# Weight stores move to the queue of loads, queries come one tile a slice, two copies go first, and loads and casts of the last stage change place

## The chip, the cores and the metric

The kernel runs on one core of one Trainium2 chip. The metric is the device time of one execution in microseconds (us). Three runs of the kernel before took 1599.2, 1599.79 and 1606.01 us; their median is 1599.79 us.

## The reference

Linear attention, and then two layers of the form "product, activation, product", all in float32:

```python
kv = einsum('bhsd,bhse->bhde', k, v)            # 8 x 8 heads, 576 positions, 64 wide
o = einsum('bhsd,bhde->bhse', q, kv)
x = o / sqrt(mean(o * o, -1) + 1e-6) * g_norm   # then 4608 tokens x 512
h = x @ moe_w_in                                # 512 x 2048
x = (h * sigmoid(h)) @ moe_w_out                # 2048 x 512
h = x @ moe2_w_in
out = (s * relu(h) ** 2 + b) @ moe2_w_out
```

The weights arrive as 64-bit floats. The kernel reads them as pairs of 32-bit integers and decodes them on ACT and DVE.

## The kernel before

Every large product is made of two float32r parts of each operand (`hi`, the cast; `lo`, the rest) and three passes: hi with hi, hi with lo, lo with hi. Four stages follow each other.

**First stage** (`emit_h`, line 470). Nine blocks of 512 tokens (j = 0 to 8), each in 16 slices (m). A slice is 12 matmuls into `ph`, a Silu on ACT (line 484), and beside them in `first_stage` the attention of block j + 1: kv products (line 349, m = 0 to 3), the transposes of the queries (`emit_qT`, line 364, m = 3 to 6), the output products and squares (`out_tile`, lines 374 to 428, m = 4 to 7), and the transposes into `xh` and `xl` (lines 442 to 447, m = 11 to 14). `load_next` (line 539) issues on SP the loads for that: four query tiles (line 357) in slices 0 and 1, keys and values of block j + 2 in slices 4 to 7. A query tile that crosses the border between two batches is loaded in two pieces.

**Weights of later stages.** From block 1 on, each slice also takes two or three steps of `weight_steps` for the weights of stages 2 and 3 (stage 4 follows during the third stage). Their products are made by the Strassen-Winograd scheme, seven products instead of eight, P1 to P7, and so each of 8 raw tiles gives seven combinations. `split` (line 228) writes a combination as `hi` (cast on ACT, line 235) and `lo` (subtraction on DVE, line 236) and puts off its store to DRAM by a slice or more with `defer` (line 237, issued by ACT). `run_late` issues what has come due. Raw weights are loaded by SP (lines 138 and 143) into two rooms, the next when its room has been decoded (`merge`, line 160).

**Second and fourth stage** (`Output`, matmuls at line 885). Five column blocks of 1024 tokens (the last, block 0, of 512), in units of one product and one quarter of the sum: 12 matmuls, six for each half q of the outputs. `load` brings tiles `r`, `sa` and `ka` of the activation from DRAM, `prepare` adds or subtracts them on DVE, `make` splits them (cast at line 808 on ACT, `lo` at line 810 on DVE), as a rule for the unit three ahead. After a product's last unit `end_of` takes the sums out of the banks. After P7 it copies y to `c` on ACT (line 860), adds v on DVE (line 861) and, in the last stage alone, scales it on ACT (`scaled`, line 821). The next product, P4, goes on in the bank y that was copied.

**Third stage** (`Hidden`, matmuls at line 677). For each of eight pairs of output tiles the seven products as slots of six matmuls, with copies and squares on ACT (lines 694 to 721) and sums on DVE; results go to `gt` in DRAM by stores that ACT issues (line 689). P4 and P3 come one pair late, so the last slots of the stage are P6, P3, P2, P7, P4, P3. `beside3` (line 963) puts beside the last block the loads of the last stage's weights (`grid[4].load`, line 312), the loads of its first activation tiles (`out4.load`) and their first casts (`out4.make`). `beside4` loads the rest of those weights, one in each unit, until 28 are there.

**What sets the order.** The order on every engine is that of the program text. An issue of a transfer stands in the stream of the engine that issues it, and can have to wait: for its data, for its room, or for the landing of an earlier transfer, as the profile's waits show. What stands behind it on that engine waits too.

Of the kernel before, what the change touches and what calls it, by code (L numbers as in the profile page):

```python
# [17 lines left out]
def kernel(  # L18
# [36 lines left out]
    nc = tc.nc  # L55
# [9 lines left out]
    TT = T // P  # L65
# [23 lines left out]
    def room(tag, shape, dtype, name):  # L89
        return sbuf.tile(shape, dtype, tag=tag, name=name)  # L90

    def bank(tag, name):
        return psum.tile([P, T], F32, tag=tag, name=name)
# [55 lines left out]
    def decode(stage, i, step):  # L149
        raw = raw_t[stage, i]  # L150
        low, high = raw[:, :, 0], raw[:, :, 1]
        if step == "rebias":
            nc.scalar.activation(high.bitcast(F32), high.bitcast(F32), AF.Copy, scale=REBIAS)
        elif step == "low":
            nc.vector.tensor_single_scalar(low, low, 29, op=ALU.logical_shift_right)
        elif step == "sign":
            nc.vector.scalar_tensor_tensor(low, high, SIGN, low, op0=ALU.bitwise_and, op1=ALU.bitwise_or)
        elif step == "merge":
            f = wf_t[stage, i] = room("wf_0", [P, WN], F32, f"wf{stage}_{i}")
            nc.vector.scalar_tensor_tensor(  # L160
                f.bitcast(I32), high, 3, low, op0=ALU.logical_shift_left, op1=ALU.bitwise_or
            )
# [25 lines left out]
    P1, P5, P6, P2, P7, P4, P3 = range(7)  # L188
    wd = {s: [[dram.tile([P, 2, T], F32, name=f"wd{s}_{k}_{a}") for a in range(NA)] for k in range(7)] for s in (2, 3, 4)}

    def quarters(stage, i):
        f = wf_t[stage, i]
        if stage % 2:
            f = f.rearrange("p (c h f) -> p c h f", c=KT, h=2)
            return f[:, 0:2, 0], f[:, 2:4, 0], f[:, 0:2, 1], f[:, 2:4, 1]
        f = f.rearrange("p (r h e) -> p r h e", r=2, h=2)
        return f[:, 0, 0], f[:, 1, 0], f[:, 0, 1], f[:, 1, 1]
# [3 lines left out]
    def weight_steps(stage, raws, sums_in, granule, slots, behind=None):  # L201

        made = {}
        turn = [0]

        def combine(i, part):
            a11, a12, a21, a22 = quarters(stage, i)
            if part == 0:
                if len(sums_in) == 1:
                    t = room(sums_in[0], [P, 4, 2 * P], F32, f"ws{stage}_{i}")  # L210
                    s = [t[:, n] for n in range(4)]
                else:
                    t = [room(tag, [P, 2, 2 * P], F32, f"ws{stage}_{i}_{tag}") for tag in sums_in]
                    s = [t[n // 2][:, n % 2] for n in range(4)]
                if stage % 2:
                    s = [x.rearrange("p (c f) -> p c f", c=2) for x in s]
                made[i] = dict(zip((P1, P2, P4, P5, P6, P7, P3), (a11, a12, a22, *s)))
                nc.vector.tensor_add(made[i][P5], a21, a22)
                nc.vector.tensor_sub(made[i][P6], made[i][P5], a11)
            elif part == 1:  # L220
                nc.vector.tensor_sub(made[i][P7], a11, a21)
                nc.vector.tensor_sub(made[i][P3], a12, made[i][P6])
            else:
                f = wf_t[stage, i].rearrange("p (r e) -> p r e", r=2)
                for r in range(2):
                    nc.vector.tensor_add(csum[0], csum[0], f[:, r])

        def split(i, k):
            src = made[i][k]
            to = granule(turn[0])  # L230
            turn[0] += 1
            hi, lo = to[:, 0], to[:, 1]
            if stage % 2:
                hi, lo = (x.rearrange("p (c f) -> p c f", c=2) for x in (hi, lo))
            nc.scalar.copy(hi, src)
            nc.vector.tensor_sub(lo, src, hi)
            defer(slots, lambda: nc.scalar.dma_start(
                wd[stage][k][i // 2][:, i % 2, :], to.bitcast(F32).rearrange("p s e -> p (s e)")
            ))

        def step(i, what):
            if i < NF:
                decode(stage, i, what)
                if what == "merge":
                    n = i + len(raws)
                    if n < NF:
                        load_raw(stage, n, raws[n % len(raws)])
                    elif behind:
                        load_raw(behind, n - NF, raws[n % len(raws)])

        def begin():
            if stage == 4:
                csum.append(room("gl_1", [P, T], F32, "csum"))
                nc.vector.memset(csum[0], 0.0)
            for i, tag in enumerate(raws):
                if (stage, i) not in raw_t:
                    load_raw(stage, i, tag)

        yield begin
        for what in ("rebias", "low", "sign", "merge"):  # L260
            yield lambda what=what: step(0, what)
        for i in range(NF):
            yield lambda i=i: combine(i, 0)
            yield lambda i=i: split(i, P1)
            yield lambda i=i: combine(i, 1)
            yield lambda i=i: split(i, P2)
            if stage == 4:
                yield lambda i=i: combine(i, 2)
            for k in (P4, P5, P6):
                yield lambda i=i, k=k: split(i, k)  # L270
            yield lambda i=i: step(i + 1, "rebias")
            yield lambda i=i: split(i, P7)
            yield lambda i=i: step(i + 1, "low")
            yield lambda i=i: split(i, P3)
            yield lambda i=i: step(i + 1, "sign")
            yield lambda i=i: step(i + 1, "merge")
# [4 lines left out]
    def defer(slots, f):  # L281
        late.append([slots, f])
# [71 lines left out]
    def load_q(t):  # L354
        a = q_pages[t % TT // 2][:, t % 2].rearrange("p (h d) -> p h d", h=H)
        for off, n, b, s in token_runs(t * P, P):
            nc.sync.dma_start(a[off:off + n], q[b, :, s:s + n, :].rearrange("h p d -> p h d"))
        q_t[t] = a
# [180 lines left out]
    def load_next(j, m):  # L539

        t0 = TT * (j + 1)
        if m < 2:
            load_q(t0 + 2 * m)
            load_q(t0 + 2 * m + 1)
        if 4 <= m < 4 + NP and j + 2 < B:
            load_kv(j + 2, m - 4)

# [188 lines left out]
    class Output:  # L736
# [109 lines left out]
        def end_of(self, b, k):  # L846
            n = size[b]
            x, y, v = ([self.acc.get((kind, q)) for q in range(2)] for kind in "xyv")
            for q in range(2):
                if k == P1:  # L850
                    self.acc["y", q] = bank(f"h_{q}", f"qy{self.stage}_{b}_{q}")
                    nc.scalar.copy(self.acc["y", q][:, :n], x[q][:, :n])
                elif k == P6:
                    self.acc["u", q] = room(U_ROOMS[q], [P, T], F32, f"qu{self.stage}_{b}_{q}")
                    nc.scalar.copy(self.acc["u", q][:, :n], y[q][:, :n])
                elif k == P2:
                    self.scaled(self.c_room(b, 0, q), x[q][:, :n], q)
                elif k == P7:
                    c = self.c_room(b, 1, 2 + q)
                    nc.scalar.copy(c, y[q][:, :n])  # L860
                    nc.vector.tensor_add(c, v[q][:, :n], c)
                    self.scaled(c, c, 2 + q)
                elif k == P4:
                    self.scaled(self.c_room(b, 0, 2 + q), y[q][:, :n], 2 + q)
                elif k == P3:
                    c = self.c_room(b, 1, q)
                    nc.vector.tensor_add(c, v[q][:, :n], self.acc["u", q][:, :n])
                    self.scaled(c, c, q)
            if self.stage == 4 and k in (P4, P3):
                self.waiting.extend((b, int(k == P3), r) for r in range(n // P))  # L870

# [46 lines left out]
    out2, hidden3, out4 = Output(2), Hidden(3), Output(4)  # L918
# [44 lines left out]
    def beside3(b, i, k):  # L963
        if b == order[0] and k in (P1, P4, P3, P7):
            grid[3].load()
        if b != order[-1]:
            if 0 < i < NF - 1 and k not in (P1, P3) and (i, k) != (NF - 2, P4):
                do_some(steps4, 1)
            return
        if i >= 3 and k in (P5, P2):  # L970
            grid[4].load()
        if i == 3 and k == P1:
            out4.load(2)
        if i == NF - 1:
            if k == P6:
                out4.load(4)
            if k in (P1, P5, P2, P7):
                out4.make({P1: 1, P5: 2, P2: 3, P7: 4}[k])

    def beside4(b, k, a):  # L980
        if b == order[0]:
# [126 lines left out]
```

## Time and profile before

| | |
|---|---|
| median of three runs | 1599.79 us |
| the profiled execution | 1600.95 us, of it 1599.2 us the span |
| granted clock of TensorE, mean | 0.997 |
| PE / DVE / ACT busy | 98% / 60% / 51% of the span |
| transfers | 349.58 MB, mean 219 GB/s |
| weight stores of stages 2 and 3 (`wd<-wo`, issued by ACT) | 112, 256 KB each, landing 3.8 us in the middle |
| query loads (`qp`, issued by SP) | 36, 28 of them of 256 KB |
| first / second / third / last stage begin at about | 36 / 528 / 877 / 1227 us |

PE is the engine that computes nearly the whole time; the other columns say how much the rest has to do beside it. In the rows, a bracket such as [2.59 <-ACT xh L446] means that the engine stood idle for 2.59 us before this instruction and that ACT's work of line 446 ended the wait. PEld is the weight load of TensorE. Names ending in q (ACTq, SPq) are an engine's issue of a transfer.

### The profile page before, as it was taken

Reading aid. Unit: us, or ns where it says so; the run is one execution under the profiler, and the core shown is the slowest. Engines: PE = TensorE matmul, PEld = TensorE weight load, DVE = VectorE, ACT = ScalarE, POOL = GpSimd, SP = SyncE. Lnnn points to the kernel's source line nnn. Section 1 sums busy time; section 2 is a strip of 40 time slices with the busy share of each in tenths; the row PEclk is TensorE's granted clock in tenths of the full one; section 3 lists DMA queues with packets and bytes.
Section 4 is the critical chain, followed back from the end, with each engine's and each line's share of the span. In section 5 each row is a group of like instructions: output and inputs, shape, how many; then the busy total and the mean of one; then the engine's idle time right before and its main releaser. Section 6 shows DMA issues by size and latency. Waiting matters only on the chain.

```text
span 1599.2 us, 21751 instructions
## 1 busy us (share of the span) xinstructions
PE 1569.1 (98%) x8232; PEld 1308.2 (82%) x8232; DVE 958.3 (60%) x1298; ACT 811.1 (51%) x1310; POOL 1.6 (0%) x8
## 2 busy tenths in 40 slices
PE   7999999999999999999999999999999999999998
PEld 4788887878888888888889788888888888888888
DVE  5635545545520758585858576767655757575845
ACT  3645554555432444444445565656555455555455
POOL 0000000000000000000000000000000000000000
PEclk9999999999999999999999999999999999999999
DMA  8977888798569763635349956574577862626251
GB/s 250 271 242 244 287 279 240 251 289 264 198 225 308 271 216 124 212 119 210 105 134 349 360 211 231 196 258 169 206 270 261 321 243 85 230 86 227 89 158 54
DMA packets 225609, 349.58 MB, mean 219 GB/s; under 512 B 56544, under 2 KB 94432, under 8 KB 225504
## 3 DMA queue, kind: packets, MB, share of 16 engines
q1 hardware_dynamic: 143936, 209.48, 40.9%
q10 hardware_dynamic: 81568, 138.71, 23.3%
q8 instruction: 65, 1.06, 0.3%
q14 instruction: 40, 0.33, 0.1%
HBM read 209.72 MB, written 138.41 MB: 218 GB/s over the span
## 4 chain that ended last, share of the span: by engine, by line
PE 88%; DMA 6%; ACT 2%; DVE 2%; issue 1%; ACTq 0%; SPq 0%; DVEq 0%
PE ph L470 23%; PE qy L885 16%; PE qx L885 12%; PE qv L885 11%; PE py L677 9%; PE pv L677 6%; PE px L677 6%; PE po L374 2%; PE pkv L349 2%; DMA r<-gt 1%; DMA w<-wd 1%; PE pt L837 1%; PE px L442 1%; DMA gt<-g 1%; PE pq L364 1%
## 5 line engine op out<-in xcount | busy, mean ns | idle before, releaser
L885 PE MATMUL qy<-o,w 128*128 128x512 f32 (+1 forms) x1440 | 300.3, 368 | 1.5 <-ACT c L860 1.5
L885 PEld LDWEIGHTS qy<-o,w 128*128 128x128 f32 x1440 | 250.8, 189 | 48.0 <-ACT c L860 3.4
L810 DVE TENSOR_TENSOR o<-ka,o 128x1024 fp32r<-128x1024 f32 (+1 forms) x160 | 178.5, 1116 | 164.0 <-ACT o L808 163.4
L808 ACT CAST o<-ka 128x1024 fp32r<-128x1024 f32 (+1 forms) x160 | 153.9, 965 | 156.7 <-PE qv L885 68.6
L885 PE MATMUL qv<-o,w 128*128 128x512 f32 (+1 forms) x960 | 203.2, 369 | 1.3 <-DVE o L810 1.3
L885 PE MATMUL qx<-o,w 128*128 128x512 f32 (+1 forms) x960 | 203.9, 370 | 0.0
L885 PEld LDWEIGHTS qx<-o,w 128*128 128x128 f32 x960 | 168.1, 190 | 29.9
L885 PEld LDWEIGHTS qv<-o,w 128*128 128x128 f32 x960 | 167.1, 189 | 31.1 <-DVE o L810 1.7
L484 ACT ACTIVATE g<-ph 128x512 f32<-128x512 f32 x144 | 86.2, 599 | 177.2 <-PE ph L470 163.9
L470 PE MATMUL ph<-xh,wh 128*128 128x512 f32 x576 | 165.7, 410 | 4.0 <-ACT xh L446 3.4
L677 PE MATMUL py<-x,w 128*128 128x512 f32 (+1 forms) x720 | 162.0, 369 | 4.2 <-ACT g L700 2.4
L470 PE MATMUL ph<-xl,wh 128*128 128x512 f32 x576 | 155.5, 392 | 0.0
L470 PE MATMUL ph<-xh,wl 128*128 128x512 f32 x576 | 154.5, 390 | 0.0
L677 PEld LDWEIGHTS py<-x,w 128*128 128x128 f32 x720 | 126.2, 188 | 28.6 <-ACT g L700 3.0
L470 PEld LDWEIGHTS ph<-xl,wh 128*128 128x128 f32 x576 | 108.6, 189 | 24.5 <-DVE xl L447 0.4
L470 PEld LDWEIGHTS ph<-xh,wl 128*128 128x128 f32 x576 | 108.2, 188 | 23.2
L470 PEld LDWEIGHTS ph<-xh,wh 128*128 128x128 f32 x576 | 101.3, 189 | 23.4 <-ACT xh L446 4.6
L808 ACT CAST o<-r 128x1024 fp32r<-128x1024 f32 (+1 forms) x80 | 77.1, 964 | 84.7 <-PE qy L885 41.3
L677 PE MATMUL pv<-x,w 128*128 128x512 f32 (+1 forms) x480 | 112.2, 369 | 0.3 <-DVE g L702 0.3
L677 PE MATMUL px<-x,w 128*128 128x512 f32 (+1 forms) x480 | 111.5, 368 | 0.0
L810 DVE TENSOR_TENSOR o<-r,o 128x1024 fp32r<-128x1024 f32 (+1 forms) x80 | 89.3, 1116 | 34.3 <-ACT o L808 34.2
L677 PEld LDWEIGHTS pv<-x,w 128*128 128x128 f32 x480 | 85.1, 190 | 15.5 <-DVE g L702 0.6
(114 smaller groups left out, 1632.9 us busy)
## 6 DMA issues: line engine op xcount, KB each, us to landing
r<-gt SPq DMA_DIRECT2D x96, 512.0 KB, 4.6
w<-wd SPq DMA_DIRECT2D x84, 512.0 KB, 6.6
gt<-g ACTq DMA_DIRECT2D x160, 256.0 KB, 2.6
gt<-g ACTq DMA_DIRECT2D x56, 512.0 KB, 3.8
wd<-wo ACTq DMA_DIRECT2D x112, 256.0 KB, 3.8
wr<-in_moe_w_in_dram SPq DMA_DIRECT2D x16, 1024.0 KB, 6.2
wr<-in_moe_w_out_dram SPq DMA_DIRECT2D x16, 1024.0 KB, 5.8
ka<-gt SPq DMA_DIRECT2D x32, 512.0 KB, 3.6
```

Of the source, the lines that this page charges most:

```text
L349: nc.tensor.matmul(ps[r, r], kc, vc, start=(c == 0), stop=(c == SC))
L364: nc.tensor.transpose(ps[:, p * P:(p + 1) * P], a[:, p * P:(p + 1) * P], ident)
L374: nc.tensor.matmul(po[off:off + n, p * P:(p + 1) * P], qT_t[t][:, p, off:off + n], kvw[b % 2][:, p, :], start=True, stop=True,)
L442: nc.tensor.transpose(ps[:, p, :], xn[:, p * P:(p + 1) * P], ident)
L470: nc.tensor.matmul(ps, wt[:, c, :], xt[:, c, :], start=(n == 0 and c == 0), stop=(n == 2 and c == KT - 1))
L484: nc.scalar.activation(g, ps, AF.Silu)
L677: nc.tensor.matmul(ps, a[:, s, c], x[t][c], start=(k in (P1, P5) and n == c == 0), stop=(n == 2 and c == 1), skip_group_check=True,)
L808: nc.scalar.copy(o[:, :, 0], x)
L810: nc.vector.tensor_sub(o[:, :, 1], x, o[:, :, 0])
L837: nc.tensor.transpose(ps[:, e * P:(e + 1) * P], self.c[b, h, e][:, r * P:(r + 1) * P], ident)
L885: nc.tensor.matmul(ps, t[:, s], self.o[u][:, i, p], start=(k in (P1, P5) and a == i == m == 0), stop=(a == NA - 1 and i == 1 and m == 2), ...
```

## The change

Four things change place; no arithmetic and no transfer is added or removed. The stores of `split` for stages 2 and 3 are issued by SP, those of stage 4 still by ACT. `load_next` loads one query tile in each of slices 0 to 3. `end_of` makes both copies of P7 first and then the sums with their scalings. In the last block of the third stage the weights of the last stage are loaded after P5 from the third pair on (6 loads, before: after P5 and P2 from the fourth on, 10), and of the four casts made ahead the first stays after P1, the second comes after P7 instead of P5, and the other two are made when the last stage starts.

```diff
--- before.py
+++ after.py
@@ -234,7 +234,8 @@
                 hi, lo = (x.rearrange("p (c f) -> p c f", c=2) for x in (hi, lo))
             nc.scalar.copy(hi, src)
             nc.vector.tensor_sub(lo, src, hi)
-            defer(slots, lambda: nc.scalar.dma_start(
+            queue = nc.scalar if stage == 4 else nc.sync
+            defer(slots, lambda: queue.dma_start(
                 wd[stage][k][i // 2][:, i % 2, :], to.bitcast(F32).rearrange("p s e -> p (s e)")
             ))
 
@@ -539,9 +540,8 @@
     def load_next(j, m):
 
         t0 = TT * (j + 1)
-        if m < 2:
-            load_q(t0 + 2 * m)
-            load_q(t0 + 2 * m + 1)
+        if m < TT:
+            load_q(t0 + m)
         if 4 <= m < 4 + NP and j + 2 < B:
             load_kv(j + 2, m - 4)
 
@@ -856,16 +856,18 @@
                 elif k == P2:
                     self.scaled(self.c_room(b, 0, q), x[q][:, :n], q)
                 elif k == P7:
-                    c = self.c_room(b, 1, 2 + q)
-                    nc.scalar.copy(c, y[q][:, :n])
-                    nc.vector.tensor_add(c, v[q][:, :n], c)
-                    self.scaled(c, c, 2 + q)
+                    nc.scalar.copy(self.c_room(b, 1, 2 + q), y[q][:, :n])
                 elif k == P4:
                     self.scaled(self.c_room(b, 0, 2 + q), y[q][:, :n], 2 + q)
                 elif k == P3:
                     c = self.c_room(b, 1, q)
                     nc.vector.tensor_add(c, v[q][:, :n], self.acc["u", q][:, :n])
                     self.scaled(c, c, q)
+            if k == P7:
+                for q in range(2):
+                    c = self.c[b, 1, 2 + q]
+                    nc.vector.tensor_add(c, v[q][:, :n], c)
+                    self.scaled(c, c, 2 + q)
             if self.stage == 4 and k in (P4, P3):
                 self.waiting.extend((b, int(k == P3), r) for r in range(n // P))
 
@@ -967,15 +969,15 @@
             if 0 < i < NF - 1 and k not in (P1, P3) and (i, k) != (NF - 2, P4):
                 do_some(steps4, 1)
             return
-        if i >= 3 and k in (P5, P2):
+        if i >= 2 and k == P5:
             grid[4].load()
         if i == 3 and k == P1:
             out4.load(2)
         if i == NF - 1:
             if k == P6:
                 out4.load(4)
-            if k in (P1, P5, P2, P7):
-                out4.make({P1: 1, P5: 2, P2: 3, P7: 4}[k])
+            if k in (P1, P7):
+                out4.make({P1: 1, P7: 2}[k])
 
     def beside4(b, k, a):
         if b == order[0]:
```

## Rows read from the trace of the kernel before

**Rows 1.** The page, busy time and share of the span of each engine.
```profile
PE 1569.1 (98%) x8232; PEld 1308.2 (82%) x8232; DVE 958.3 (60%) x1298; ACT 811.1 (51%) x1310; POOL 1.6 (0%) x8
```
**Rows 2.** Windows: stretch, length, busy of PE, PEld, DVE, ACT, POOL; clock; DMA; GB/s.
```profile
640.00:660.00 20.00, 20.00 (x90) 16.56 (x89) 12.91 (x13) 10.00 (x12) 0.00 (x0) 1.00 0.35 109
...
260.00:280.00 20.00, 17.41 (x131) 12.95 (x129) 5.42 (x8) 6.64 (x15) 0.00 (x0) 0.91 0.85 235
...
1220.00:1240.00 20.00, 17.37 (x83) 14.45 (x82) 15.46 (x18) 9.29 (x17) 0.00 (x0) 0.91 1.01 368
```
**Rows 3.** Chain in order of time, first stage: start, length, what.
```profile
180.37 10.91 PE ph L470 x48
...
297.00 10.93 PE ph L470 x48
...
354.18 10.91 PE ph L470 x48
...
409.59 11.11 PE ph L470 x48
```
**Rows 4.** Timeline of ACT: start, length, work; in brackets idle before, and its releaser.
```profile
257.95 4.44 ACTq L237 DMA_DIRECT2D wd<-wo  x3
...
351.40 0.60 ACT L382 ACTIVATE sq<-po 128x512 f32<-128x512 f32 x1 [3.43 <-DMA wd<-wo]
```
**Rows 5.** Timeline of PE at the same two places.
```profile
263.17 2.07 PE L470 MATMUL ph<-xh,wh 128*128 128x512 f32 x4 [2.59 <-ACT xh L446]
...
353.02 1.16 PE L374 MATMUL po<-at_kvw 128*128 128x128 f32 x8 [1.60 <-ACT at_kvw L366]
```
**Rows 6.** Tile qp, its loads' landing; timelines of DVE and PE, block 6.
```profile
DMA to landing us min/median/max: 3.0/7.3/12.5
...
382.31 0.42 DVE L236 TENSOR_TENSOR wo<-wf,wo 128x256 fp32r<-128x256 f32 x1
...
392.94 0.66 PE L364 MATMUL pq<-ident,qp 128*128 128x128 f32 x4
```
**Rows 7.** Timelines of DVE, SP and PE, first block.
```profile
44.83 1.23 DVE L160 SCALAR_TENSOR_TENSOR wf<-wr 128x1024 int32<-128x1024 int32 x1
...
49.11 3.41 SPq L138 DMA_DIRECT2D wr<-in_moe_w_in_dram  x2
...
57.25 0.69 DVE L155 TENSOR_SCALAR wr<-wr 128x1024 int32<-128x1024 int32 x1 [5.16 <-DMA wr<-in_moe_w_in_dram]
...
59.91 1.16 PE L374 MATMUL po<-kvw,at_kvw 128*128 128x128 f32 x8 [0.76 <-ACT at_kvw L366]
```
**Rows 8.** DMA issues (KB each, median us to landing); timelines, end of third stage.
```profile
w<-wd SPq DMA_DIRECT2D x84, 512.0 KB, 6.6
...
1185.57 12.71 SPq L312 DMA_DIRECT2D w<-wd  x9
...
1200.37 0.98 PE L677 MATMUL py<-x,w 128*128 128x256 f32 x6 [1.10 <-ACT u L721]
...
1218.36 2.00 ACT L808 CAST o<-ka 128x1024 fp32r<-128x1024 f32 x2 [0.78 <-DVE g L703]
...
1221.47 0.98 PE L677 MATMUL py<-x,w 128*128 128x256 f32 x6 [0.69 <-ACT u L721]
1224.04 0.98 PE L677 MATMUL py<-x,w 128*128 128x256 f32 x6 [1.60 <-ACT g L700]
...
1226.62 6.78 PE L885 MATMUL qx<-o,w 128*128 128x512 f32 x24
...
1234.05 5.75 PE L885 MATMUL qx<-o,w 128*128 128x512 f32 x24
...
1228.38 1.23 DVE L790 TENSOR_TENSOR ka<-r,ka 128x1024 f32<-128x1024 f32 x1 [0.64 <-DMA r<-gt]
```
**Rows 9.** Timeline of ACT, last stage; the page's group of the `qy` matmuls.
```profile
1284.30 0.56 ACT L860 COPY c<-qy 128x512 f32<-128x512 f32 x1
...
L885 PE MATMUL qy<-o,w 128*128 128x512 f32 (+1 forms) x1440 | 300.3, 368 | 1.5 <-ACT c L860 1.5
```

## The prediction

> **What bounds the kernel now.** The first view is the page's busy times: PE is busy for 98% of the span and DVE and ACT for 60 and 51% [rows 1]. So a change that adds and removes no matmul can win only PE's gaps, some 30 us, and what the clock loses behind them. The second view, busy time by windows, says where they lie: in the second stage PE has all of its 20 us; around 260 us it has 17.41 and around 1220 us 17.37, and in both windows the granted clock falls to 0.91, a part of the window at the lower of TensorE's two levels (1.2 instead of 2.4 GHz) after PE had stood [rows 2]. Third, the chain in order of time gives each block of the first stage a marker, its run of 48 matmuls of `ph`: blocks that follow each other cleanly are 55.4 us apart (354.18 to 409.59), but 180.37 to 297.00 is 116.63 for two, 5.8 too many, and 297.00 to 354.18 is 57.18, 1.8 too many [rows 3]. So the first stage loses 7.6 us beside its start. Fourth, ACT's timeline says to what: the weight stores of line 237 stand in ACT's own stream. Three of them held it for 4.44 us, and one made the `sq` behind it wait 3.43 us for an earlier transfer's landing [rows 4]; PE then waited 2.59 us for `xh` and 1.60 us for `at_kvw`, both made by ACT behind those stores [rows 5].
>
> **Weight stores to SP's queue.** 2 stages x 8 raw tiles x 7 combinations are 112 stores; none is added. On ACT each took an issue and its wait; on SP the same two things hold only SP. What ACT has left to store in these blocks is one `gt` in two slices. The two gaps of PE go if ACT runs on: 2.59 + 1.60, and the slow clock behind the first: four matmuls took 2.07 us there [rows 5] against some 1.15 at 0.23 to 0.29 us each (24 in 5.75 us [rows 8], 48 in 10.91 with their overlap [rows 3]), and the next eight were slow for a while too, together an estimated 1.5 to 2. That is 5.7 to 6.2 directly and 7.6 by the markers. The transfers don't get shorter, though, and a `gt` store can meet the same late landing. Bounds 0 and 7.6; I take 5.0, near the upper end because both long waits of ACT were at line 237 and none at the `gt` issue.
>
> Behind a waiting store on SP stand the loads: queries, keys and values, raw weights. Keys and values are loaded a block ahead and raw weights two tiles ahead: their cover is tens of us. The queries have the least.
>
> **Queries one tile a slice.** Five or four issues in slices 0 and 1 become one or two in each of slices 0 to 3; the bytes are the same. Tile m is then loaded in slice m and used in slice m + 3. In the tightest block I read, the store ahead of tile 0 has its data at 382.73 and PE transposes the tile at 392.94: 10.2 us for a load that lands after 3.0 to 12.5 us, 7.3 in the middle [rows 6]. So cost 0, with 2.9 us to spare; the other end is rival 2.
>
> In the first block this order helps. The raw tile that SP issued at 49.11, behind five queries, could have gone when line 160 freed its room at 46.06; it landed at 57.25, DVE stood 5.16 us for it and PE 0.76 [rows 7]. With two queries fewer ahead it goes up to 3 us earlier, more than the 0.76: **0.8** gained, bounds 0 and 0.8.
>
> **Loads of the last stage's weights.** The last half block of the third stage issues 6 of them instead of 10; 4 move behind units 18 to 21 of the last stage. Now nine go out within 12.71 us, and PE then waits 1.10 us for `u` (ACT's `gt` store stands for one of those loads) [rows 8]. With six the crowd is a third smaller: I take 0.7 of the 1.10, bounds 0 and 1.1. The lead shrinks from 10 units to 6; a unit is 12 matmuls, 2.9 us by [rows 8] at most, so 16 to 17 us, while such a load lands in 6.6 us in the middle [rows 8]. Cost 0.
>
> **Casts of the last stage.** Now two casts stand at 1218.36 (2.00 us) ahead of ACT's work for the last products, and by the code a third, which needs a `ka` tile whose room comes free only then, stands between those products' copies; PE waits 0.69 for `u` and 1.60 for `g` [rows 8]. From 1221.47, the start of the third product from the end, to 1226.62, the start of the last stage, pass 5.15 us with three half-width products of some 0.7 us (six matmuls of half 0.23): 3.05 lost, with the 0.69 before it 3.7. Then the first 24 matmuls take 6.78 us instead of 5.75: 1.0 to the slow clock. After the change one cast stands after P1 and one after P7; the two that wait for `ka` come when the last stage starts. What stays is the copy between P7 and P4 with its handovers: a full-width copy is 0.56 [rows 9], I take 0.8. Gain 3.7 - 0.8 + 1.0 = **3.9**, bounds 1.3 (rival 3) and 4.7. With the 0.7: 4.6.
>
> What is late next: casts 3 and 4 now run beside units 0 and 1, 5.5 us. DVE puts the subtraction for unit 4 between their two `lo` parts, and that waits for an `r` load. Even if it began no earlier than now, at 1228.38 [rows 8], the second `lo` part would end at 1228.38 + 2 x 1.23 = 1230.8, and unit 3 starts at 1226.62 - 2.9 + 3 x 2.73 [rows 3] + 0.7 for the small `psums` matmuls (from 1226.62 + 6.78 to 1234.05 [rows 8]) = 1232.6: free by 1.8 us.
>
> **Both copies ahead of the sums.** In the last stage the second copy stands behind the first half's sum and scaling and ends late; PE waits for it five times, 1.5 us in all, and nothing else makes this group wait [rows 9]. With both copies first it starts when its product is done, while PE runs the next unit's first six matmuls: **1.4**, bounds 1 and 1.5. In the second stage the scaling doesn't exist and PE has no gap [rows 2]: 0, covered by the same six matmuls.
>
> **Sum.** 5.0 + 0.8 + 4.6 + 1.4 = 11.8. The profiled execution is 1600.95 (span 1599.2), 1.2 above the median of the runs, 1599.79; the sum counts gaps, so I take it from the median: **1588.0 us** (-0.7%). A measurement of this kernel tells about 0.5%, 8.0 us, from no change: the borders are 1591.8 and 1607.8.
>
> **Rivals.**
> 1. *The wait stays with ACT.* The landings that were late are late still, and the next store on ACT, a `gt`, meets them; now it also can wait for a store that SP holds. Then the first stage wins nothing: 1588.0 + 5.0 = 1593, within 0.5%. For it: ACT waits for landings [rows 4], not for the issue itself, and these don't change. Against: ACT has a third of the stores it had. The Trainium skill's DMA: Bandwidth & Descriptors (Issuing engines are not separate DMA queues) says that transfers of all engines run on the same 16 DMA engines and that another issuing engine saves only the issue's own time; by that rule alone this rival's 1593 is what comes out, and the trace agrees as far as ACT's waits end with landings. Chance 0.20.
> 2. *Queries come late, and the kernel is slower.* A store that waits on SP as three did on ACT, 4.44 us [rows 4], leaves a query 10.2 - 4.4 = 5.8 us; by the middle landing of 7.3 it is 1.5 late, by the longest 6.7 [rows 6], and PE stands at its transpose in each of the six blocks that have stores. At the mean, 4.1 a block, that is 25 us against 6.8 won elsewhere: 1599.8 + 18 = 1618. It decides from (8.0 + 6.8) / 6 = 2.5 us a block. Against: only two or three long holds stood in six blocks, and one query a slice lands sooner than a crowd of five. The Trainium skill's Perfetto Trace Analysis (DMA Optimizations) advises one issuing engine for inputs and another for outputs, which the change gives up; no run yet shows what that costs here. Chance 0.06.
> 3. *The start of the last stage gives back its gain.* Casts 3 and 4 now stand on ACT behind the third stage's last `gt` stores, at a time when the transfers fill their engines (share 1.01 [rows 2]). A store held there for more than the 1.8 us of slack makes unit 2 or 3 late by the rest; held as long as the three were, 4.44 [rows 4], it costs 2.6 of the 3.9, and 1590.6 comes out. For it: the crowd at just this place. Against: no PE wait now falls behind these stores. Chance 0.14.
>
> **Numbers.** The forecast has 0.60. The low end takes every term at its upper bound: 7.6 + 0.8 + 4.7 + 1.1 + 1.5 = 15.7, 1584; the high end takes in rival 1 with half of the last stage's gain, 1595.5. Outside are rival 2 and mixtures below. Faster: the forecast, and most of rival 3 and a little of rival 1 and its mixtures, 0.71. Within 0.5%: most of rival 1 and rests of the others, 0.22. Slower: rival 2 and a rest, 0.07.
>
> **What would show it.** Right: no wait of ACT at line 237 in the first stage, markers 55.4 us apart throughout, no PE gap over 1 us between 90 and 440 us, clock 1.00 there; the first matmul of the last stage about 1 us behind the last of the third at full clock; no idle of `qy` for `c`. Rival 1: ACT waits for landings at line 493 and PE gaps behind them. Rival 2: PE idle at `pq`, released by a `qp` transfer, in several blocks. Rival 3: PE idle in the last stage's units 2 to 4, DVE waiting for `r<-gt` just before. If the first stage keeps over 5 us of gaps, or the last stage's first matmuls still run at 1.2 GHz, the prediction is wrong at that step.

## The result, and the profile after

The changed kernel takes **1586.07 us** (median of four runs, 1585.16 to 1589.41) against 1600.27 us for the kernel before beside it: ratio 0.9907, interval 0.9889 to 0.9925, so 0.9% faster. The forecast was 1588.0 us, the range 1584 to 1595.5. The profiled execution took 1585.16 us, its span 1583.3: 15.9 less than the span of before.

The page's busy times, the issues of the moved stores and the group of the `qy` matmuls answer to [rows 1, 9] and to the table's line on the stores:

```profile
PE 1562.5 (99%) x8232; PEld 1306.5 (83%) x8232; DVE 958.7 (61%) x1298; ACT 810.1 (51%) x1310; POOL 1.6 (0%) x8
...
L887 PE MATMUL qy<-o,w 128*128 128x512 f32 (+1 forms) x1440 | 298.9, 368 | 0.0
...
wd<-wo SPq DMA_DIRECT2D x112, 256.0 KB, 3.7
```

Every engine has as many instructions as before. `qy` no longer waits for `c`, and a store lands in 3.7 us as it did in 3.8: the transfers have not become faster.

The chain's markers in the first stage, against [rows 3] (start, length, what):

```profile
179.01 10.93 PE ph L471 x48
...
289.89 10.93 PE ph L471 x48
...
345.19 10.93 PE ph L471 x48
...
400.63 11.11 PE ph L471 x48
```

Two blocks now take 110.88 us (before 116.63) and the next 55.30 (before 57.18): all blocks follow each other cleanly. The two windows that [rows 2] showed with a fallen clock:

```profile
260.00:280.00 20.00, 20.00 (x159) 15.86 (x158) 5.87 (x11) 8.83 (x21) 0.00 (x0) 1.00 0.76 225
...
1220.00:1240.00 20.00, 20.00 (x94) 16.67 (x93) 17.93 (x16) 9.26 (x11) 0.00 (x0) 1.00 1.04 401
```

PE has all of its 20 us in both, at 1.00. Where the third stage ends and the last begins, PE's timeline (against [rows 8]; in brackets idle before and its releaser):

```profile
1191.34 0.98 PE L677 MATMUL py<-x,w 128*128 128x256 f32 x6 [0.51 <-ACT u L721]
...
1212.98 0.98 PE L677 MATMUL py<-x,w 128*128 128x256 f32 x6 [0.50 <-ACT g L700]
...
1214.51 5.63 PE L887 MATMUL qx<-o,w 128*128 128x512 f32 x24
```

Of the 1.10 us of idle in the half block 0.51 are left, of 0.69 + 1.60 + 0.34 in the last products 0.50, and the first 24 matmuls of the last stage take 5.63 us instead of 6.78.

By markers of the two chains, the 15.9 us of span came from these places:

| stretch | change, us |
|---|---|
| start, to the ninth slice of block 0 (69.52 to 68.18) | -1.3 |
| first stage from there (two blocks 5.75, the third 1.88, the last 0.4) | -8.0 |
| second stage | 0 |
| passage to the third stage and its body | +0.9 |
| end of the third stage and the last stage's first units | -4.8 |
| rest of the last stage | -2.6 |

The parts add to 15.8; the spans differ by 15.9. The +0.9 is scatter as far as the runs tell: from the second stage's first matmul to the 1200th of the third pass 620.1 us in the kernel before, 621.0 in the changed one, and 619.2 to 622.5 in the runs below.

### The profile page after: what moved, and what is told of

It is laid out like the page before. It is cut to its first block, busy times and chain, and to the rows that moved or that the text cites. A ratio compares the mean times of both kernels' runs of the same rounds, so it can differ in the third digit from the quotient of the medians.

```text
span 1583.3 us, 21805 instructions
## 1 busy us (share of the span) xinstructions
PE 1562.5 (99%) x8232; PEld 1306.5 (83%) x8232; DVE 958.7 (61%) x1298; ACT 810.1 (51%) x1310; POOL 1.6 (0%) x8
## 4 chain that ended last, share of the span: by engine, by line
PE 92%; DMA 4%; DVE 1%; ACT 1%; issue 1%; SPq 0%; ACTq 0%; DVEq 0%
PE ph L471 25%; PE qy L887 18%; PE qx L887 11%; PE qv L887 11%; PE py L677 9%; PE px L677 6%; PE pv L677 6%; PE po L375 2%; PE pkv L350 2%; PE pq L365 1%; DMA r<-gt 1%; PE px L443 1%; PE pt L837 1%; DMA wd<-wp 1%; DMA kv<-in_v_dram 1%
## 5 line engine op out<-in xcount | busy, mean ns | idle before, releaser
L677 PEld LDWEIGHTS px<-x,w 128*128 128x128 f32 x480 | 84.8, 189 | 15.1
```

The lines of the kernel that those rows point to most:

```text
L677: nc.tensor.matmul(ps, a[:, s, c], x[t][c], start=(k in (P1, P5) and n == c == 0), stop=(n == 2 and c == 1), skip_group_check=True,)
```

## The experiments

Twelve kernels ran. A run's own kernel before is in its row, because the runs were on several chips. The ratio and its 95% interval come from the single runs and are not the quotient of the two medians.

| run | kernel | us | before, us | ratio and interval |
|---|---|---|---|---|
| e1_stores | before, stores on SP | 1593.13 | 1602.55 | 0.9944 (0.9927 to 0.9960) |
| e2_queries | before, queries one a slice | 1600.38 | 1602.55 | 0.9995 (0.9984 to 1.0006) |
| e3_stores_queries | before, both of these | 1594.29 | 1602.55 | 0.9951 (0.9936 to 0.9965) |
| e4_ends | before, copies first | 1599.20 | 1602.55 | 0.9982 (0.9973 to 0.9992) |
| e5_loads | before, loads moved | 1602.74 | 1601.64 | 1.0003 (0.9994 to 1.0013) |
| e6_casts | before, casts moved | 1598.11 | 1601.64 | 0.9974 (0.9963 to 0.9984) |
| e7_late_queries | after, queries two slices later | 1609.51 | 1601.64 | 1.0044 (1.0027 to 1.0060) |
| e8_half | after, stage 3's stores on ACT | 1588.73 | 1601.64 | 0.9920 (0.9905 to 0.9934) |
| e9_all_sp | after, stage 4's stores on SP too | 1586.99 | 1601.98 | 0.9917 (0.9903 to 0.9932) |
| e10_g_sp | after, first stage's `gt` stores on SP too | 1586.86 | 1601.98 | 0.9908 (0.9895 to 0.9921) |
| e11_changed | after itself | 1586.63 | 1601.98 | 0.9911 (0.9898 to 0.9925) |
| e12_later_weights | after, stage 4's weights begun later | 1584.64 | 1601.37 | 0.9899 (0.9881 to 0.9917) |

The parts alone, e3, e4, e5 and e6, give -8.3, -3.4, +1.1 and -3.5, together -14.0 us; the whole gives -14.2 and, in e11, -15.4. So, as far as medians can tell, they hardly touch each other.

### Stores and queries, each alone and both

```diff
-            defer(slots, lambda: nc.scalar.dma_start(
+            queue = nc.scalar if stage == 4 else nc.sync
+            defer(slots, lambda: queue.dma_start(
```

> The kernel before with the store queue alone: the stores of stages 2 and 3 are issued by SP, the queries still come in slices 0 and 1. Theory A (ACT was held by its own waiting stores): the whole 8.0 us that the first stage won between its second and its eighth marker come back here, markers 55.3 to 55.6 us apart, no wait of ACT at the stores; about 1592 us. Theory B (the gain came from spreading the queries over four slices): at most 2 us of the 8.0, the gaps near 231 to 268 us stay; about 1598. Rival 2 of the prediction (loads late behind stores) would show here first, with five queries crowded behind stores: PE idle at pq released by a qp transfer, over 1 us in some block.

```diff
-        if m < 2:
-            load_q(t0 + 2 * m)
-            load_q(t0 + 2 * m + 1)
+        if m < TT:
+            load_q(t0 + m)
```

> The kernel before with one query tile a slice alone, stores still on ACT. Theory A: the start wins 0.8 to 1.3 us (the raw tile of line 138 goes out about 3 us earlier, no gap of PE near 59.9 us); the gaps of blocks 3 and 5, 5.8 and 1.8 us by the markers, may move but stay over 4 us in sum; about 1598.5. Theory B: they go without the stores being moved; about 1591.

> Stores on SP and queries one tile a slice, the rest as before. Theory A: 1.3 us at the start and 8.0 in the first stage, together 9.4 at the start of the second stage, which begins near 519.1 us; about 1591. If the two parts need each other, this is more than 1 us faster than the store queue and the query order add up to.

Chain of e1, first stage:

```profile
181.45 10.93 PE ph L471 x48
...
292.33 10.93 PE ph L471 x48
347.64 10.93 PE ph L471 x48
403.08 11.11 PE ph L471 x48
```

The same chain of e2:

```profile
181.89 10.91 PE ph L470 x48
299.52 10.93 PE ph L470 x48
356.49 10.95 PE ph L470 x48
411.97 11.11 PE ph L470 x48
```

The stores alone make the stage clean: two blocks in 110.88 us, then 55.31 and 55.44. The queries alone leave it as it was or worse: 117.63 for two, 56.97 for the next. (e2's trace is of the slowest of its ten executions, 1606.20 us against a median of 1600.38, so "worse" may be scatter.) From the ninth slice of block 0 to the second stage pass 458.98 us in the kernel before, 451.07 in e1, 461.44 in e2, 451.00 in e3, 450.97 in the changed kernel. The whole gain of this stage is the stores'. The queries gain only in the start: from the first `ph` to the ninth slice 33.44 us before, 32.13 in e2, 32.47 in e3, 32.41 after, against 33.39 in e1, about 1 us. In the other runs it is 32.11 to 32.44 with one tile a slice (e8 to e12) and 32.98 to 34.40 with two (e4 to e6). SP's and DVE's timelines of the changed kernel show the raw tile of [rows 7]:

```profile
45.81 0.81 SPq L138 DMA_DIRECT2D wr<-in_moe_w_in_dram  x1
...
52.58 0.70 DVE L155 TENSOR_SCALAR wr<-wr 128x1024 int32<-128x1024 int32 x1 [0.81 <-DMA wr<-in_moe_w_in_dram]
```

It goes out 3.3 us earlier (at 49.11 before), DVE waits 0.81 us for it instead of 5.16, and PE's wait of 0.76 is gone. In the medians of e1 and e3 that doesn't show: e3, expected at about 1591, came at 1594.29, beside a kernel before of 1602.55 (1600.27 in the result). Its start and first stage are as expected, but its last stage is longer, 356.23 us from the first `qv` to PE's end where the kernel before has 354.89; why stays open.

How a store held PE shows in a place of the kernel before that the prediction had not read. ACT's timeline, then PE's:

```profile
238.93 0.33 ACTq L237 DMA_DIRECT2D wd<-wo  x1
239.30 0.60 ACT L382 ACTIVATE sq<-po 128x512 f32<-128x512 f32 x1 [3.90 <-DMA gt<-g]
...
241.54 1.20 PE L470 MATMUL ph<-xh,wh 128*128 128x512 f32 x4 [0.40 <-ACT g L484]
```

ACT stood for 3.90 us with a store at the head of its stream; that an earlier `gt` transfer ended the wait doesn't make it a wait of the `gt` issue. PE shows 0.40 us of idle here, but between the `ph` matmuls at 238.26 and 247.91 the kernel before falls behind the changed one by 1.1 us: 0.7 at this stop, and 0.4 at a second one at 244.69, whose 0.14 us of idle is too short for a bracket.

All waits of ACT for transfers between 90 and 440 us, by the view of waits, are 31.8 us in 13 waits before, 2.1 in one in e1, 4.3 in two after. In nine of the 13, 23.3 us in sum, an issue of line 237 goes out at the end of the wait and ACT's next work begins right behind it, whatever transfer is named; all nine are gone in e1 and in the changed kernel. The other four, and the ones that are left, are of another kind, as the changed kernel's ACT shows:

```profile
292.68 0.60 ACT L485 ACTIVATE g<-ph 128x512 f32<-128x512 f32 x1 [1.38 <-PE ph L471]
...
295.40 0.60 ACT L485 ACTIVATE g<-ph 128x512 f32<-128x512 f32 x1 [2.12 <-DMA gt<-g]
```

The two Silu start 2.72 us apart, the time that the 12 `ph` matmuls of a slice take (236.91 to 239.63), so ACT would have waited as long for PE; the other four of the kernel before have the same distance. Of PE the view lists no wait there in e1, e3 and the changed kernel. What became of the stores' waits, in the changed kernel (view of waits of SP and ACT from 90 to 440: line, releaser, us in total, times, longest):

```profile
SPq L238 <- DVE wo L236: 111.2, 63, 4.4
SPq L238 <- DVE ws_v L221: 42.0, 12, 8.3
...
ACT g L485 <- DMA gt<-g: 4.3, 2, 2.1
```

SP stands for 111 us until DVE has made what it is to store. Those waits cost PE nothing.

### Half of the stores back, and further stores to SP

```diff
-            queue = nc.scalar if stage == 4 else nc.sync
+            queue = nc.sync if stage == 2 else nc.scalar
```

> The changed kernel with the stores of stage 2's weights on SP and those of stage 3's back on ACT. Stage 2's stores fill blocks 1 to 3, stage 3's blocks 4 to 6. Theory A (the loss sits where stores wait on ACT, block by block): blocks 1 to 3 stay clean (55.3 to 55.6 us by the markers of slice 8, the one from block 3 to block 4 too), blocks 4 to 6 lose 1 to 3 us in sum again. Theory B (the loss comes of the sum of transfers, and the queue only shifts it): gaps of 2 us or more appear in blocks 1 to 3 as well.

Stage 2's weights come first: in e8 SP issues their stores from 106 to 261 us and ACT those of stage 3 from 278 to 432 us. The chain of e8:

```profile
180.41 10.93 PE ph L471 x48
...
291.30 10.93 PE ph L471 x48
348.30 10.95 PE ph L471 x48
```

and, at the place where it becomes unclean, ACT's and PE's timelines:

```profile
345.15 0.33 ACTq L238 DMA_DIRECT2D wd<-wo  x1
345.52 0.60 ACT L383 ACTIVATE sq<-po 128x512 f32<-128x512 f32 x1 [3.26 <-DMA wd<-wo]
...
347.14 1.16 PE L375 MATMUL po<-at_kvw 128*128 128x128 f32 x8 [1.43 <-ACT at_kvw L367]
```

Clean to 291.30 (110.89 for two blocks), then 57.00: 1.7 us too many, with a store at the head of ACT's wait and PE idle behind it, as [rows 4, 5] had it at 351 and 353. The loss comes back in the stretch to which the stores came back and nowhere earlier; over the whole stage it is 453.24 us against 450.97.

```diff
-            defer(1, lambda: nc.scalar.dma_start(to, both))
+            defer(1, lambda: nc.sync.dma_start(to, both))
```

> The changed kernel with the first stage's activation stores on SP too, so that ACT issues nothing there. If ACT's remaining issues still cost something, up to 1 us faster; by the markers nothing is left to win, so the first stage stays at 451.0 us from the first block's ninth slice to the second stage. What decides about slower: each such store waits for a Silu of its slice, and the loads behind it come later; if a query lands after its transpose, PE idle at pq as in the run with late queries, 1 to 7 us a block.

e10 has this at all three `gt` stores of the first stage. It passes the stage in 450.97 us, the changed kernel's time: no query came late, and nothing was left to win. The view lists no wait of ACT for a transfer there, and the 4.3 us that it listed in the changed kernel were worth nothing.

### How near the queries are to being late

```diff
-        if m < TT:
-            load_q(t0 + m)
+        if 2 <= m < TT + 2:
+            load_q(t0 + m - 2)
```

> The changed kernel with the queries two slices later still (tile m in slice m + 2), to price rival 2. In the changed kernel the loads are issued 10 to 12 us before PE needs the tile and land after 3.4 to 8.1 us; two slices are 7.6 us, so most would land 1 to 5 us late. Theory of rival 2: PE idle at pq behind qp transfers in all eight blocks, 2 to 4 us a block with the slow clock behind it, 16 to 32 us in sum: 1602 to 1618. If a late query is absorbed (SP runs ahead of PE far enough, or later slices take up the delay): under 3 us in sum.

In e7 each query comes two slices later than in the changed kernel, some 7.7 us (a slice with kv products takes 3.84, as the `ph` matmuls at 268.52 and 272.36 of the kernel before show). The view of PE's waits:

```profile
PE pq L365 <- DMA qp<-in_q_dram: 14.7, 8, 4.1
```

and the window with the longest of the seven that lie between 90 and 440 us (2.38 us, at 250.31):

```profile
240.00:260.00 20.00, 17.62 (x88) 14.83 (x87) 9.51 (x23) 9.72 (x21) 0.00 (x0) 0.91 0.83 260
```

This is rival 2's mechanism, made to happen: PE idle at `pq` eight times (the longest, 4.1 us, in the start), from the ninth slice of block 0 to the second stage 465.66 us instead of 450.97, and the kernel slower than before. So the changed kernel's queries land early enough, but by less than 7.7 us at the tightest places. By the landings and transposes in the traces the least time between the two is 2.4 us there, 1.8 in the kernel before. The changed kernel's SP in one block:

```profile
204.82 1.10 SPq L238 DMA_DIRECT2D wd<-wo  x2
206.01 0.82 SPq L358 DMA_DIRECT2D qp<-in_q_dram  x1
207.79 2.28 SPq L238 DMA_DIRECT2D wd<-wo  x2
210.55 0.38 SPq L358 DMA_DIRECT2D qp<-in_q_dram  x1
```

and, over the whole kernel, its tile `qp`:

```profile
DMA to landing us min/median/max: 3.4/6.2/9.6
```

Stores and queries alternate; the stores hold SP for one to two us, and a query lands in 6.2 us in the middle and 9.6 at most (the expectation above had put 8.1), where [rows 6] had 7.3 and 12.5.

### The copies

```diff
                 elif k == P7:
-                    c = self.c_room(b, 1, 2 + q)
-                    nc.scalar.copy(c, y[q][:, :n])
-                    nc.vector.tensor_add(c, v[q][:, :n], c)
-                    self.scaled(c, c, 2 + q)
+                    nc.scalar.copy(self.c_room(b, 1, 2 + q), y[q][:, :n])
...
+            if k == P7:
+                for q in range(2):
+                    c = self.c[b, 1, 2 + q]
+                    nc.vector.tensor_add(c, v[q][:, :n], c)
+                    self.scaled(c, c, 2 + q)
```

> The kernel before with the copies of P7 ahead of the sums alone. By the idle of the matmul rows it wins 1.5 us (0.24 in each of four full blocks, 0.49 in the half one); by the markers of the changed kernel, where the starts of P7's successors moved by 0.53 us in each full block and 0.75 in the half one, it wins 2.6 to 2.9. The difference is what PE loses around a gap, beyond the idle that its row shows. The second stage keeps its length to 0.1 us. About 1597.5, within the scatter of the times: the markers decide.

The chain of the kernel before through P7 and P4 of a full block:

```profile
1272.44 8.17 PE qy L885 x36
1284.92 9.82 PE qy L885 x42
1294.74 5.44 PE qv L885 x24
```

and of e4, a full block and the half block:

```profile
1272.55 21.76 PE qy L887 x96
...
1571.24 11.53 PE qy L887 x96
```

The 96 `qy` matmuls took 1294.74 - 1272.44 = 22.30 us and take 21.76: 0.54 in each of four full blocks, where the rows of before showed 0.24 of idle. In the half block 12.28 become 11.53, 0.75 where 0.51 showed. Together 2.9 us, and e4's median is 3.4 lower. The changed kernel has the same two lengths, but its chain has a wait behind the first:

```profile
1259.18 21.76 PE qy L887 x96
1280.94 5.44 PE qv L887 x24
1287.96 5.77 DMA out_dram<-out
```

From 1280.94 to the second `qx` part behind it pass 19.37 us, before 18.98 (from 1294.74 to 1313.72): some 0.4 us of the 2.9 went back at this wait. Why it came isn't tested.

### Loads and casts, each alone

```diff
-        if i >= 3 and k in (P5, P2):
+        if i >= 2 and k == P5:
             grid[4].load()
```

> The kernel before with the fewer and earlier loads of the last stage's weights alone (6 instead of 10 in the third stage's last half block). Theory A (the loads' crowd holds ACT at one gt store): the gap of PE in that half block, 1.1 us before, falls to 0.5 and the stretch from the 1200th matmul of the third stage to the last stage's P5 goes from 91.2 to 90.6 us; the gaps of the last products stay. Theory B (the crowd also makes the ka tiles late, and this is what costs at the last products): that stretch falls to 88 us or less. The last stage itself keeps its length: no PE wait for a weight tile.

```diff
-            if k in (P1, P5, P2, P7):
-                out4.make({P1: 1, P5: 2, P2: 3, P7: 4}[k])
+            if k in (P1, P7):
+                out4.make({P1: 1, P7: 2}[k])
```

> The kernel before with the later casts of the last stage alone. Theory A (two casts, and a third that waits for its tile, stand on ACT before the copies the last products need): the stretch from the 1200th matmul of the third stage to the last stage's P5 falls by 4.2 us, from 91.2 to 87.0; the first matmuls of the last stage run at the full clock; the gap of 1.1 us in the half block stays. Theory B: by 1.5 or less. Rival 3 of the prediction would show as PE idle in units 2 to 4 of the last stage.

PE's timeline of e5:

```profile
1193.32 0.98 PE L677 MATMUL py<-x,w 128*128 128x256 f32 x6 [0.19 <-ACT u L721]
...
1222.83 1.65 PE L677 MATMUL py<-x,w 128*128 128x256 f32 x6 [2.27 <-ACT g L700]
```

and of e6:

```profile
1200.63 0.98 PE L677 MATMUL py<-x,w 128*128 128x256 f32 x6 [1.00 <-ACT u L721]
...
1222.28 0.98 PE L677 MATMUL py<-x,w 128*128 128x256 f32 x6 [0.46 <-ACT g L700]
1223.81 5.63 PE L885 MATMUL qx<-o,w 128*128 128x512 f32 x24
```

Each edit takes away its own gap and leaves the other's: the loads 1.10 to 0.19, the casts the gap of the last products and the slow first matmuls. From the 1200th matmul of the third stage to the last stage's first `qv` pass 91.24 us before, 90.29 in e5, 87.03 in e6, 86.43 in the changed kernel. The loads' 0.95 is too small for e5's interval.

### A gap that the change leaves

At 905 us, in the third stage, PE waits for `g` in every one of these kernels (0.80 us before, 1.40 after, 1.74 in e11). In the changed kernel ACT stands there at a cast (line 235) of stage 4's weights. Either a store on ACT holds it, or the cast waits until an earlier store has landed and freed its room.

```diff
-            queue = nc.scalar if stage == 4 else nc.sync
-            defer(slots, lambda: queue.dma_start(
+            defer(slots, lambda: nc.sync.dma_start(
```

> The changed kernel with the stores of stage 4's weights on SP too. These run beside the third stage, whose only gap of PE behind a store in the changed kernel is 1.4 us near 905 us. Theory A (ACT stands at the issue): the gap goes, 1 to 2 us faster than the changed kernel. Theory B (ACT stands at a cast whose room, one of three, is still being stored: the landing took 9.76 us): the queue makes no difference, within 0.5 us, or worse, since a store on SP now stands behind 512 KB loads.

> The changed kernel itself, on the chip of the next two, to compare with them and to narrow the ratio: 0.9907 again within 0.002.

```diff
-            if 0 < i < NF - 1 and k not in (P1, P3) and (i, k) != (NF - 2, P4):
+            first = b == order[0]
+            if first < i < NF - 1 and k not in (P1, P3) and (i, k) != (NF - 2, P4) or i == 0 and not first and k in (P5, P6):
                 do_some(steps4, 1)
```

> The changed kernel with the preparation of stage 4's weights begun one pair of tiles (9.5 us) later in the third stage's first block, and the five steps lost there made up in the first pairs of the later blocks. By theory B of the run before (a cast waits for the landing of a store in the crowd of loads near 895 to 905 us) the gap of 1.4 to 1.7 us there goes or shrinks to under 0.5, and the stage is 1 to 2 us shorter. If the crowd lasts longer than one pair, the gap only moves later by some 9 us and nothing is won.

ACT's timeline of the changed kernel:

```profile
904.53 0.41 ACT L235 CAST wp<-ws 128x256 fp32r<-128x256 f32 x1 [2.08 <-DMA wd<-wp]
```

the transfer that its chain has just before this cast:

```profile
894.75 9.76 DMA wd<-wp
```

ACT's timeline of e9, where SP issues the store:

```profile
904.60 0.40 ACT L235 CAST wp<-ws 128x256 fp32r<-128x256 f32 x1 [2.52 <-DMA wd<-wp]
```

and of e12:

```profile
909.81 0.41 ACT L235 CAST wp<-ws 128x256 fp32r<-128x256 f32 x1 [0.77 <-DMA wd<-wp]
```

In e9 the wait stays whoever issues, so it is the room's: the cast waits for the landing of an earlier store. PE still waits 1.5 us, and the median is e11's within 0.4 us. In e12 the first casts come one pair later, the wait is 0.77 and PE has none between 880 and 930 us. Between the 120th and the 1200th matmul of the third stage pass 244.80 us instead of 246.91 and, in e11, 247.34. e12 is the lowest time of the study; its 1.4 to 2.0 us below the changed kernel lie inside the intervals of the ratios, so the trace shows the gain and the medians don't settle it.

## Why the prediction was right

**The forecast held**, by 1.9 us, with every sign right and the terms of the stores and the copies too small. Point by point:

- **Stores to SP: 5.0 predicted, 8.0 measured** (e1: 7.9), beyond the upper bound of 7.6. The mechanism was right: waits behind a store in ACT's stream, gone with the stores (e1) and back with half of them (e8). The step that failed is the discount, "a `gt` store can meet the same late landing": no wait of ACT stands at a `gt` issue in the changed kernel's first stage, and e10 shows that nothing was left to win there. The bound itself missed 0.4, because it was read from blocks to 409.59 alone. And the direct count of 5.7 to 6.2 missed the place at 239, where PE lost 1.1 us and its rows show a bracket of 0.40.
- **Queries: 0.8 predicted, about 1.0 measured** in the start, 0 elsewhere, as said. The cover held: the least time between landing and transpose is 2.4 us, where 2.9 was worked out for one block.
- **Loads and casts: 0.7 + 3.9 = 4.6 predicted, 4.8 measured.** Alone they give 0.95 and 4.2; together the loads keep 0.6 (1.10 to 0.51). The copy that stays between P7 and P4 shows 0.50 us of idle and cost 0.76 (the products' starts at 1211.60, 1212.98 and 1213.80 against 0.72 apart where PE runs on), so its 0.8 was right.
- **Copies: 1.4 predicted, 2.9 measured**, 2.6 net. The step that failed is the upper bound of 1.5: it took the recorded idle as the loss, and the loss was 0.54 for 0.24 and 0.75 for 0.51. The second stage gained nothing, as predicted.
- **The sum**: 11.8 predicted, 14.2 measured, by the median of the kernel before beside it. That the forecast is within 1.9 us is in part luck: by the table's markers the four gains add to 16.7, more than all upper bounds together (15.7). The 0.9 of scatter in the middle takes some of it back, and the traced executions lie further apart than the medians (1600.95 is above the median of its kernel, 1585.16 the lowest of four).

**Rival 1** (the wait stays with ACT, 1593) did not come: ACT's nine waits behind its own stores, 23.3 us in the first stage, are gone, and none came at the `gt` issue there. The Trainium skill's DMA: Bandwidth & Descriptors (Issuing engines are not separate DMA queues) says first that transfers of all issuing engines run on the same 16 DMA engines; the trace agrees: the same bytes pass and a store lands in 3.7 us for 3.8. Its second half, that another issuing engine saves the issue's time alone, falls short here, because an issue that has to wait holds all that stands behind it in its engine's stream; that was worth 8 us.

**Rival 2** (late queries, 1618) has its price from e7: 1609.51 with queries 7.7 us later, 23 us over the changed kernel in eight blocks. PE stood 1.8 us a wait and the kernel lost 2.9 a block, where the prediction had put 4.1. The Trainium skill's Perfetto Trace Analysis (DMA Optimizations) says that it may make sense to issue inputs on one engine and outputs on another; e1, e3 and e10 mix them on SP and pass the first stage in 451 us, the cleanest here. What decides by these runs is what stands behind the waiting issue, not the direction of the transfer.

**Rival 3** (the last stage's start gives back) did not come. In the changed kernel's DVE timeline the fourth `lo` part ends 1219.34 + 1.22 = 1220.56, and the four units' matmuls run without a gap to 1226.54; unit 3 began at about 1220.79 + 2.9 = 1223.7, free by 3.1 us where 1.8 was worked out.

## What to carry to other kernels

An issue of a transfer belongs on an engine whose stream has nothing urgent behind it: look not at what an issue costs but at what its wait can hold, and then count the cover of what stands behind it in the new place, as the queries' cover here. Where the computing engine never rests, bound a gap's cost by markers of equal work on both sides of it, since the recorded idle is only its lower end (below). And put the steps that need freed rooms behind the copies that the computing engine waits for.

## What the runs showed that was not expected

- Recorded idle of PE undercounts a short stop: 0.24 us of idle cost 0.54, 0.51 cost 0.75, and at 241 us 0.40 cost 0.7, all at a granted clock of 1.00 in the windows read. The single matmuls of the trace show why. Where PE runs on before the stop at 1284.92, a matmul's row is 0.39 us long, but the next one starts 0.23 us after it, so idle is counted some 0.16 us too late. Behind the stop the next start comes after 0.34 us instead of 0.23. Both add to the 0.24, with a little more in the starts that follow.
- The first `ph` of the first stage starts at 35.52 us in the changed kernel and at 36.79 in e11, the same program. So gains of about 1 us in the start can't be read from its end alone.
- A wait that ends with a transfer of one tile can belong to the issue of another: of the nine waits behind stores in the kernel before, four (11.4 us) have `gt<-g` as releaser, and they went away in e1, where only the `wd` stores left ACT.
